# A planned mLSTM-and-two-layers kernel: another cutting of its first steps, two banks, one copy on another engine, other planner numbers

## The chip, the cores and the metric

The kernel runs on one core of one Trainium2 chip. The metric is the device time of one execution in microseconds, the median of several runs. Times inside the execution come from one profiled execution, counted from the start of its span.

## The reference

Three parts follow one another. An mLSTM attention (4 batches, 8 heads, 768 tokens, head size 40) is written as a recurrence over time; its output is a matrix of 3072 tokens by 320. Two feed-forward layers, 320 to 2048 to 320, follow, each with its own function between the two products. Gates and weights are scaled up by 8 to 64 in the inputs.

```python
for t in range(S):
    m_new = np.maximum(f_gate[:, :, t] + m, i_gate[:, :, t])
    f_stab = np.exp(f_gate[:, :, t] + m - m_new)
    i_stab = np.exp(i_gate[:, :, t] - m_new)
    m = m_new
    C = f_stab[:, :, None, None] * C + i_stab[:, :, None, None] * np.einsum('bhd,bhe->bhde', vt, kt)
    n = f_stab[:, :, None] * n + i_stab[:, :, None] * kt
    h_tilde = np.einsum('bhde,bhe->bhd', C, qt)
    nq = np.einsum('bhd,bhd->bh', n, qt)[:, :, None]
    y[:, :, t] = o * h_tilde / np.maximum(np.abs(nq), 1.0)

def _moe_ref(x, w_in, w_out):
    h = x @ w_in
    return ((h - np.tanh(h)) @ w_out).astype(np.float32)

def _moe2_ref(x, w_in, w_out):
    h = x @ w_in
    g = np.where(h >= 1, h, np.where(h <= -1, 0.0, (h + 1) ** 2 / 4))
    return (g @ w_out).astype(np.float32)
```

## The kernel before, in words

**Jobs.** The attention is cut into 24 jobs, each 128 tokens of one batch with all 8 heads (function `job`, L428). In a job the two halves of the heads are called u = 0 and 1. For each half a scan on VectorE (L489 for the first four jobs, L497 for the others) builds the decay matrix d from decay rows; from the fifth job on these rows are loaded by DMA from DRAM into the tile `fb`. The scan of the later jobs works in two diagonal blocks of 64; GpSimd copies one (L500), clears its place and fills the block below the diagonal. TensorE makes the scores of both halves into two PSUM banks (`t_s`, L516), VectorE multiplies them by d (L541), TensorE multiplies by the values and by the carried state C (`t_n`, L568 and L577), the result is normalised to x, transposed on TensorE (`t_x`, L606), and split for the layers into a high part (ScalarE, L656 and L660) and the rest (VectorE, L657 and L661). For the first four jobs a plain copy `xf` is kept as well (L642). For every fourth job the sigmoid of the o gate (L552) needs another table on ScalarE than the exponentials and tanh do.

**Layers.** Tokens go in six blocks of 512, the hidden width in 16 steps f of 128. In the first layer `step` (L689) multiplies the weights with x into a bank `h` (two banks, tag h), `activate` (L715) makes tanh on ScalarE (L725), the subtraction on VectorE (L726), the cast `gh` on ScalarE (L738) and the rest `gl` on VectorE (L739); `second` (L743) multiplies them with the second weights into four accumulators `a`, two steps later (LAG). Products are made from high and low parts (L707, L759). Only the first six steps of the first block (`WIDE`) use unsplit weights `wf` and x `xf` in one pass (L697), with the subtraction at L721. Steps zero and one of that block are issued in two column parts, 384 (the first three jobs) and 128 (the fourth); the later ones in one part of 512.

**Weights.** Each weight block of 704 columns comes as a load of 704 KB (`w64`) and is converted on ScalarE (L331) and VectorE (L333, L335), then split (L342, L344); that of the wide steps is split only later (`W_LATE`).

**What sets the order.** `Plan.schedule` is a list scheduler. Every instruction has a priority number (for the layers about the index of its step, for the jobs set by JOB0, AHEAD and others), a cost, and a margin that makes it count as finished later (LATE, or `margin` for a load). It takes what can start first, and by priority among what can start within PATIENCE; NEAR and FAR are the assumed delays from one engine to another. The result is a fixed order for each engine's queue. All loads go out on SyncE's queue (L296), in this order too. Where TensorE would wait in the planner's view, up to the end of step zero, it issues filler matmuls into a bank that nobody reads (`spare`, L853). PSUM banks are handed out by tag in the order in which the planner asks: for the later jobs `f` and `s0`, `s1` become the banks named in `jbank`, among them tn and tb, which the scores, t_x and others share in turn. A bank is free when its last reader is done.

## Time and profile before

| | us |
|---|---|
| median of 3 runs | 804.93 |
| lowest and highest | 803.73, 806.21 |
| profiled execution, its own time | 806.27 |
| span of that execution | 804.5 |
| TensorE busy (matmuls) in the span | 796.5 |
| VectorE, ScalarE, GpSimd busy | 556.8, 426.7, 201.1 |

Durations and starts below are from the profiled execution; its own time lies 1.8 us above its span. In a row of the timeline stand the start, the duration, the engine, the line and operation, output and input tiles with their partitions and elements, the number of instructions that were joined, and in brackets the idle time before with what ended it. The ends of matmuls are modelled, so two neighbours can overlap a little. In a list of waits stand, for an engine and line, what it waited for, and then the total, the number and the longest. TensorE's granted clock is 1.00 throughout, its higher level.

### The profile page before, as it was taken

To read this page: it belongs to the slowest core of one execution; us is meant where nothing else is said; L and a number is where in the kernel's file an instruction comes from. 1 tells how busy PE (TensorE), PEld (TensorE's weight loads), DVE (VectorE), ACT (ScalarE), POOL (GpSimd) and SP (SyncE) were. 2 spreads that over 40 slices of the span, in tenths; PEclk is the share of its full clock that TensorE was granted. 3 is DMA by queue.
4 is the path that set the end of the run, shared out by engine and by line. 5 is a ranking of instruction groups with operands and counts; after the bars stand their busy time and mean duration, and the time that the engine had idled before them with its cause. 6 is when DMAs were issued, how large, how long until landed. Compare 5 with 4: busy or idle time off the path is not lost.

```text
span 804.5 us, 15535 instructions
## 1 busy us (share of the span) xinstructions
PE 796.5 (99%) x6048; PEld 695.4 (86%) x6048; DVE 556.8 (69%) x931; ACT 426.7 (53%) x812; POOL 201.1 (25%) x268
## 2 busy tenths in 40 slices
PE   9999999999999999999999999999999999999998
PEld 6667889888988999889999898888989888898887
DVE  7998998888878888775456674746646566564644
ACT  4975685766776665443445543524435244342423
POOL 3245433656446554533100200200201002000000
PEclk9999999999999999999999999999999999999999
DMA  8998348887788576540543210100200000000000
GB/s 272 314 247 232 120 124 243 238 244 205 217 231 221 162 187 199 160 113 20 184 103 98 76 33 0 40 34 1 71 2 1 34 0 1 34 1 1 34 1 33
DMA packets 51300, 91.09 MB, mean 113 GB/s; under 512 B 5980, under 2 KB 33820, under 8 KB 51228
## 3 DMA queue, kind: packets, MB, share of 16 engines
q1 hardware_dynamic: 51180, 90.08, 39.4%
q8 instruction: 47, 0.77, 0.4%
q14 instruction: 25, 0.20, 0.1%
q10 hardware_dynamic: 48, 0.03, 0.0%
HBM read 76.26 MB, written 13.84 MB: 112 GB/s over the span
## 4 chain that ended last, share of the span: by engine, by line
PE 92%; DMA 3%; DVE 2%; ACT 2%; issue 0%; POOL 0%; POOLq 0%; DVEq 0%; ACTq 0%
PE a L759 40%; PE h L707 39%; DMA w<-in_w_dram 2%; PE t_n L577 2%; PE h L684 2%; PE t_c L613 2%; PE t_n L568 1%; PE t_s L537 1%; PE t_s L516 1%; PE spare L853 1%; PE t_f L477 1%; PE t_x L606 1%; DMA fb<-fr_d 1%; DVE w L344 1%; DVE w L333 0%
## 5 line engine op out<-in xcount | busy, mean ns | idle before, releaser
L707 PE MATMUL h<-x,w 128*128 128x512 f32 x1392 | 344.4, 396 | 0.7 <-DVE gl L739 0.7
L759 PE MATMUL a<-w,gh 128*128 128x320 f32 x1488 | 333.6, 311 | 0.0
L707 PEld LDWEIGHTS h<-x,w 128*128 128x128 f32 x1392 | 254.5, 188 | 58.3 <-issue 8.4
L759 PEld LDWEIGHTS a<-w,gh 128*128 128x128 f32 x1488 | 251.5, 188 | 6.8 <-issue 0.3
L759 PE MATMUL a<-w,gl 128*128 128x320 f32 x744 | 230.3, 310 | 0.0
L730 DVE TENSOR_SCALAR g<-h 128x512 f32<-128x512 f32 x96 | 65.8, 686 | 110.4 <-PE h L707 110.4
L732 ACT ACTIVATE g<-g,half 128x512 f32<-128x512 f32 x96 | 69.5, 724 | 136.8 <-DVE g L730 136.4
L759 PEld LDWEIGHTS a<-w,gl 128*128 128x128 f32 x744 | 139.7, 188 | 0.3
L823 POOL TENSOR_TENSOR x<-xl,x 128x512 fp32r<-128x512 f32 x18 | 26.8, 1512 | 275.2 <-ACT x L814 275.2
L726 DVE TENSOR_TENSOR h<-h,g 128x512 f32<-128x512 f32 x90 | 62.3, 693 | 32.7 <-ACT g L725 32.6
L725 ACT ACTIVATE g<-h 128x512 f32<-128x512 f32 x90 | 53.9, 599 | 56.8 <-PE h L707 56.5
L738 ACT CAST gh<-g 128x512 fp32r<-128x512 f32 x96 | 59.1, 616 | 46.1 <-DVE g L734 36.4
L739 DVE TENSOR_TENSOR gl<-g,gh 128x512 fp32r<-128x512 f32 x96 | 73.2, 782 | 10.7 <-ACT gh L738 10.7
L734 DVE TENSOR_TENSOR g<-h,g 128x512 f32<-128x512 f32 x96 | 65.5, 684 | 20.3 <-ACT g L732 20.3
L739 DVE TENSOR_TENSOR gl<-h,gh 128x512 fp32r<-128x512 f32 x90 | 61.1, 681 | 15.5 <-ACT gh L738 14.9
L738 ACT CAST gh<-h 128x512 fp32r<-128x512 f32 x90 | 52.3, 582 | 32.2 <-DVE h L726 23.3
L534 POOL TENSOR_TENSOR xf<-qkraw,xf 120x1024 fp32r<-120x1024 f32 x12 | 29.2, 2434 | 61.4 <-ACT xf L532 54.3
L497 DVE TENSOR_TENSOR_SCAN d<-fb,scan_id 128x256 f32<-128x256 f32 x40 | 34.3, 865 | 5.9 <-DMA fb<-fr_d 5.8
L532 ACT ACTIVATE xf<-qkraw,cs 120x512 fp32r<-120x512 f32 x48 | 32.5, 718 | 10.2 <-PE t_s L537 8.4
L541 DVE TENSOR_TENSOR d<-t_s,d 128x512 f32<-128x512 f32 x48 | 32.1, 681 | 5.9 <-PE t_s L537 5.0
L500 POOL COPY d<-d 64x256 f32<-64x256 f32 x40 | 21.5, 538 | 50.8 <-DVE d L497 48.0
L331 ACT ACTIVATE cvb<-w,half 128x704 bf16<-128x704 int8 x32 | 30.1, 941 | 4.5 <-DVE w L333 3.5
(113 smaller groups left out, 793.4 us busy)
## 6 DMA issues: line engine op xcount, KB each, us to landing
w<-in_w_dram SPq DMA_DIRECT2D x32, 703.6 KB
nat<-in_nat_dram SPq DMA_DIRECT2D x24, 484.0 KB
qkraw<-in_qk_dram SPq DMA_DIRECT2D x24, 480.0 KB
w_d<-w SPq DMA_DIRECT2D x16, 352.0 KB
w<-w_d SPq DMA_DIRECT2D x16, 352.0 KB
fb<-fr_d SPq DMA_DIRECT2D x40, 128.0 KB
qkraw<-in_qk_dram SPq DMA_DIRECT2D x24, 160.0 KB
xr_d<-xo SPq DMA_DIRECT2D x24, 160.0 KB
```

Of the source, the lines that this page charges most:

```text
L497: op("DVE", dve(512), p, lambda o=dk[u][0], i=f[u][0]: nc.vector.tensor_tensor_scan(out=o()[:, 0:HU * HL], data0=i(), data1=half_id, initi ...
L532: op("ACT", act(512, 1), at(u - 1), lambda raw=raw, t=t, z=z, cols=cols: nc.scalar.activation(t[:, cols], raw[:, cols], AF.Copy, scale=cs[ ...
L541: op("DVE", dve(512), at(2 + u), lambda p=sp[u], d=dk[u][0]: nc.vector.tensor_tensor(out=view(d()), in0=view(p.t, True), in1=view(d()), op ...
L707: op("PE", pe(n), prio, lambda i=i, c=c, s=s: nc.tensor.matmul(p[:, :n], w[:, c:c + 128], x[:, s, :n], start=(i == 0 and not layer), stop= ...
L725: op("ACT", act(n), prio + 0.5 - FFN, lambda: nc.scalar.activation(t[:, :n], p[:, :n], AF.Tanh), [p], [t])
L726: op("DVE", dve(n), prio + 0.5 - FFN, lambda: nc.vector.tensor_tensor(out=p[:, :n], in0=p[:, :n], in1=t[:, :n], op=ALU.subtract), [p, t], [p])
L730: op("DVE", dve(n), prio + 0.5 - FFN, lambda: nc.vector.tensor_scalar(t[:, :n], p[:, :n], -1.0, 1.0, op0=ALU.max, op1=ALU.min), [p], [t])
L732: op("ACT", act(n, 1), prio + 0.5 - FFN, lambda: nc.scalar.activation(t[:, :n], t[:, :n], AF.Square, bias=half[:, 0:1], scale=0.5), [t, "h ...
L734: op("DVE", dve(n), prio + 0.5 - FFN, lambda: nc.vector.tensor_tensor(out=t[:, :n], in0=p[:, :n], in1=t[:, :n], op=ALU.max), [p, t], [t])
L738: op("ACT", act(n), prio + 1 - FFN, lambda: nc.scalar.copy(gh[:, :n], y[:, :n]), [y], [gh])
L739: op("DVE", dve(n), prio + 1 - FFN, lambda: nc.vector.tensor_tensor(out=gl[:, :n], in0=y[:, :n], in1=gh[:, :n].bitcast(F32), op=ALU.subtra ...
L759: op("PE", pe(DM) if gl is not None else 2 * pe(DM, 128, 2), prio, lambda A=A, r=r, a=a, c=c, i=i, dt=dt: nc.tensor.matmul(A[:, 0:DM], a[: ...
```

## The change

Step zero of the first layer's first block is issued in three column parts (0 to 256, 256 to 384, 384 to 512), steps one and two in two (384 and 128). Steps two and three write the banks tn and tb, taken once after the fourth job's last use, instead of the two h banks. The copy of the diagonal block (L500) is made by ScalarE, at a slightly later priority. Loads of a job may be issued four steps ahead of it (LOADS) instead of two; the wide steps' weights are split two steps earlier (W_LATE) in priority, the first conversion starts one earlier (W_CONV); the assumed delay to TensorE and GpSimd's lateness are smaller (FAR, LATE); second-layer weights count as landing later, and the jobs' loads have a margin of 1600 from the seventh job on instead of 2500 from the ninth.

```diff
-AHEAD, LOADS = 7, 2
+AHEAD, LOADS = 7, 4
-SPLIT = 2
-W_LATE = 15
+CUTS = ((2, 3), (3,), (3,))
+HX = {2: 'tn', 3: 'tb'}
+W_LATE = 13
-W_CONV = [-14, -10, -7, -5, -3, -2, -1]
+W_CONV = [-15, -10, -7, -5, -3, -2, -1]
-    NEAR, FAR, PE_OUT = 80.0, 160.0, 170.0
+    NEAR, FAR, PE_OUT = 80.0, 130.0, 170.0
-    LATE = {"POOL": 0.3, "DVE": 0.05, "ACT": 0.1}
+    LATE = {"POOL": 0.2, "DVE": 0.05, "ACT": 0.1}
...
-             704, w=[t], rows=5629, margin=3000.0 if layer else 0.0)
+             704, w=[t], rows=5629, margin=6000.0 if layer else 0.0)
...
-        load(ld, lambda: nt.t, lambda: nat[b, c * L:(c + 1) * L], 484, w=[(nt, 0), (nt, 1), (nt, 2)], rows=3872, margin=2500.0 if n >= 8 else 0.0)
+        load(ld, lambda: nt.t, lambda: nat[b, c * L:(c + 1) * L], 484, w=[(nt, 0), (nt, 1), (nt, 2)], rows=3872, margin=1600.0 if n >= 6 else 0.0)
...
-            op("POOL", 380, p + 0.25, lambda ds=ds: nc.gpsimd.tensor_copy(ds()[HL:128, 1], ds()[HL:128, 0]), [Z], [D_C])
+            op("ACT", act(256), p + 0.3, lambda ds=ds: nc.scalar.copy(ds()[HL:128, 1], ds()[HL:128, 0]), [Z], [D_C])
...
-        p = None if layer else bank("h", "h")
+        p = None if layer else free.pop((k, f), None) or bank("h", "h")
         if wide(layer, k, f):
             w, x = wf[f], xf[0]
-            cut = BLK[0] - 1 if f < SPLIT else 0
-            for a, b in ((0, cut), (cut, BLK[0])) if cut else ((0, BLK[0]),):
+            cuts = (0, *(CUTS[f] if f < len(CUTS) else ()), BLK[0])
+            for a, b in zip(cuts, cuts[1:]):
                 for i in range(3):
...
     jobs(0)
+    free.update({(0, f): bank(t, "h") for f, t in HX.items()})
```

The line with `nat` stands for the same edit on `fb`, `gb` and `q3`. Lines of the changed kernel are one higher than those of the kernel before, from about L878 two.

The first place is TensorE's order from the last scores of the fourth job (`t_s`) on; `spare` are the fillers, `h_...` with `wf_284` is step zero, with `wf_386` step one, `t_x` the transposes of the third job and then of the fourth. Before (the pair of weight load and filler stands here once, and is there eight times):

```order
L516 MATMUL t_s_445<-qkraw_198 128x128
L853 LDWEIGHTS gh_88
L853 MATMUL spare_101<-gh_88 128x512
...
L606 MATMUL t_x_480<-cs_72,x_107 128x128 x3
L577 MATMUL t_n_494<-nat_211,d0_389 32x41 x32
L613 MATMUL t_c_531<-nat_211 120x123 x2
L697 MATMUL h_539<-xf_334,wf_284 128x384 x2
L606 MATMUL t_x_550<-cs_72,x_107 128x128 x3
L697 MATMUL h_539<-xf_334,wf_284 128x384
L697 MATMUL h_562<-xf_334,wf_386 128x384
L697 MATMUL h_539<-xf_334,wf_284 128x128 x3
...
L697 MATMUL h_589<-xf_334,wf_470 128x512 x3
```

And in the changed kernel:

```order
L517 MATMUL t_s_445<-qkraw_199 128x128
...
L854 MATMUL spare_101<-gh_88 128x512
L698 MATMUL h_470<-xf_334,wf_284 128x256 x3
...
L607 MATMUL t_x_485<-cs_72,x_107 128x128 x3
L578 MATMUL t_n_492<-nat_211,d0_389 32x41 x32
L614 MATMUL t_c_529<-nat_211 120x123 x2
...
L698 MATMUL h_470<-xf_334,wf_284 128x128 x3
L698 MATMUL h_546<-xf_334,wf_386 128x384
L607 MATMUL t_x_551<-cs_72,x_107 128x128 x3
...
L698 MATMUL h_577<-xf_334,wf_473 128x384 x3
```

The first 256 columns of step zero moved ahead of the third job's transposes, between two fillers where there were eight; the next 128 follow them, the last 128 follow those of the fourth.

The second place is VectorE's order at the seventh job (job six, counted from zero). `d_...<-fb_...` is a scan, `t_x` the split of the job before, `h` the subtraction after tanh, `d_...<-t_s_...` the multiplication of the scores. Before:

```order
L497 SCALAR_TENSOR_TENSOR d_1073<-fb_978,scan_id_73 128x256
L657 TENSOR_TENSOR x1_893<-t_x_1060,x1_893 128x2x128
L661 TENSOR_TENSOR x1_893<-t_x_1060,x1_893 64x128
L726 TENSOR_TENSOR h_1034<-h_1034,g_1081 128x512
L335 SCALAR_TENSOR_TENSOR w32_864<-w64_721,w32_864 128x704
L497 SCALAR_TENSOR_TENSOR d_1114<-fb_1025,scan_id_73 128x256
L541 TENSOR_TENSOR d_980<-t_s_1099,d_980 128x512
L739 TENSOR_TENSOR gl_1129<-h_1034,gh_1110 128x512
```

And in the changed kernel:

```order
L727 TENSOR_TENSOR h_1014<-h_1014,g_1049 128x512
L498 SCALAR_TENSOR_TENSOR d_1077<-fb_937,scan_id_73 128x256
L658 TENSOR_TENSOR x1_882<-t_x_1065,x1_882 128x2x128
L662 TENSOR_TENSOR x1_882<-t_x_1065,x1_882 64x128
L345 TENSOR_TENSOR w10_1026<-w32_781,w10_1026 128x704
L336 SCALAR_TENSOR_TENSOR w32_933<-w64_734,w32_933 128x704
L542 TENSOR_TENSOR d_1021<-t_s_1100,d_1021 128x512
L740 TENSOR_TENSOR gl_1130<-h_1014,gh_1084 128x512
L345 TENSOR_TENSOR w11_1123<-w32_933,w11_1123 128x704
L542 TENSOR_TENSOR d_1077<-t_s_1099,d_1077 128x512
...
L498 SCALAR_TENSOR_TENSOR d_1199<-fb_1073,scan_id_73 128x256
```

The multiplication of job six's first half (L542, d_1021) stood behind the first scan of job seven (L497, d_1114), and now stands ahead of it; the subtraction moved ahead of the other scan.

The third place is SyncE's queue of loads ahead of that. Before, `w64_929` is the last first-layer weight block, `fb_978` the decay rows of job six's second half and `fb_1025` those of job seven's first:

```order
L296 DMA fb_883<-fr_d_78 64x2x256
...
L296 DMA nat_910<-in_nat_dram 128x968
L296 DMA w64_929<-in_w1_dram 128x5629
L296 DMA fb_978<-fr_d_78 64x2x256
L296 DMA fb_978<-fr_d_78 64x256
L296 DMA q3_989<-in_q3_dram 120x384
L296 DMA qkraw_999<-in_qk_dram 40x1024 x2
L296 DMA fr_1018<-in_fg_dram 32x128
L296 DMA fb_1025<-fr_d_78 64x2x256
```

In the changed kernel the same are `w64_995`, `fb_937` and `fb_1073`, and `w64_1042` is the first second-layer block:

```order
L297 DMA nat_924<-in_nat_dram 128x968
L297 DMA fb_937<-fr_d_78 64x2x256
L297 DMA fb_937<-fr_d_78 64x256
...
L297 DMA q3_983<-in_q3_dram 120x384
...
L297 DMA w64_995<-in_w1_dram 128x5629
L297 DMA fr_1028<-in_fg_dram 32x128
...
L297 DMA w64_1042<-in_w2_dram 128x5629
L297 DMA fb_1073<-fr_d_78 64x2x256
```

The weight block moved behind the decay rows of job six, and a second-layer block moved ahead of those of job seven.

## Rows read from the trace of the kernel before

**Rows 1.** Page, busy time, share of the span and instructions of each engine.
```profile
PE 796.5 (99%) x6048; PEld 695.4 (86%) x6048; DVE 556.8 (69%) x931; ACT 426.7 (53%) x812; POOL 201.1 (25%) x268
```
**Rows 2.** Windows: length, busy us of each engine (instructions), clock, DMA share, GB/s.
```profile
40.00:50.00 10.00, 10.00 (x43) 5.70 (x42) 9.87 (x12) 7.70 (x13) 5.26 (x8) 1.00 0.80 202
60.00:70.00 10.00, 9.41 (x53) 7.08 (x52) 8.84 (x19) 5.67 (x14) 6.58 (x11) 1.00 1.03 270
70.00:80.00 10.00, 9.11 (x116) 7.83 (x117) 7.25 (x16) 6.32 (x16) 4.42 (x7) 1.00 0.77 195
500.00:600.00 100.00, 100.00 (x562) 88.17 (x562) 58.98 (x88) 41.51 (x67) 9.39 (x6) 1.00 0.09 30
```
**Rows 3.** Timeline of TensorE, 25 to 38 us: start, us, instructions, [idle before].
```profile
25.48 1.90 PE L853 MATMUL spare<-gh 128*128 128x512 bf16 x8
...
35.10 2.84 PE L697 MATMUL h<-xf,wf 128*128 128x512 f32 x6 [0.21 <-DVE gh L721]
37.78 2.32 PE L759 MATMUL a<-wf,gh 128*128 128x320 f32 x8
```
**Rows 4.** Timeline of VectorE, 24 to 51 us.
```profile
24.27 1.06 DVE L335 SCALAR_TENSOR_TENSOR wf<-w,wf 128x704 int32<-128x704 int32 x1
...
34.36 0.68 DVE L721 TENSOR_TENSOR gh<-h,g 128x512 f32<-128x512 f32 x1
...
48.59 2.41 DVE L344 TENSOR_TENSOR w<-wf,w 128x704 fp32r<-128x704 f32 x1
```
**Rows 5.** TensorE's list of waits, whole run: total us, times, longest.
```profile
PE spare L853 <- POOL gh L856: 1.3, 1, 1.3
...
PE h L697 <- DVE gh L721: 0.2, 1, 0.2
```
**Rows 6.** Timeline of TensorE, 67 to 121 us, its four larger waits.
```profile
67.05 1.25 PE L516 MATMUL t_s<-qkraw 40*128 40x128 f32 x16 [0.59 <-issue]
...
79.75 1.25 PE L516 MATMUL t_s<-qkraw 40*128 40x128 f32 x16 [0.85 <-issue]
...
83.42 0.87 PE L568 MATMUL t_n<-C,q 120*128 120x123 f32 x6 [0.69 <-POOL d L500]
...
119.14 2.11 PE L707 MATMUL h<-x,w 128*128 128x512 f32 x8 [0.65 <-DVE gl L739]
```
**Rows 7.** Timeline of VectorE, 65 to 84 us.
```profile
65.05 0.69 DVE L497 TENSOR_TENSOR_SCAN d<-fb,scan_id 128x256 f32<-128x256 f32 x1 [1.08 <-DMA fb<-fr_d]
...
66.67 0.28 DVE L661 TENSOR_TENSOR x<-t_x,x 64x128 fp32r<-64x128 f32 x1
...
78.34 0.69 DVE L497 TENSOR_TENSOR_SCAN d<-fb,scan_id 128x256 f32<-128x256 f32 x1 [1.16 <-DMA fb<-fr_d]
...
79.36 0.28 DVE L661 TENSOR_TENSOR x<-t_x,x 64x128 fp32r<-64x128 f32 x1
...
82.04 0.69 DVE L497 TENSOR_TENSOR_SCAN d<-fb,scan_id 128x256 f32<-128x256 f32 x1 [0.70 <-DMA fb<-fr_d]
82.65 0.67 DVE L541 TENSOR_TENSOR d<-t_s,d 128x512 f32<-128x512 f32 x1
```
**Rows 8.** Timeline of ScalarE, 64 to 119 us.
```profile
64.88 0.37 ACT L656 CAST x<-t_x 128x256 fp32r<-128x256 f32 x1 [0.27 <-PE t_x L606]
...
115.29 1.28 ACT L552 ACT_TABLE_LOAD   x1
...
117.78 0.57 ACT L738 CAST gh<-h 128x512 fp32r<-128x512 f32 x1
```
**Rows 9.** Timeline of SyncE's DMA issues, 67 to 72 us.
```profile
67.64 0.36 SPq L296 DMA_DIRECT2D w<-in_w_dram  x1
70.57 1.25 SPq L296 DMA_DIRECT2D fb<-fr_d  x2
```
**Rows 10.** Page, costliest groups: busy us, mean ns, idle before with its releaser.
```profile
L500 POOL COPY d<-d 64x256 f32<-64x256 f32 x40 | 21.5, 538 | 50.8 <-DVE d L497 48.0
```
**Rows 11.** VectorE's list of waits, 40 to 130 us.
```profile
DVE d L497 <- DMA fb<-fr_d: 4.7, 5, 1.2
```

More of the change, by code (lines that the diff above doesn't have):

```diff
@@ L451, in job @@
                              "w h t -> w (h t)").unsqueeze(0).to_broadcast([HL, w, HU * HL]),
-                         kb, r=[("fr_d", kc, v) for v in ((0, 1) if a == 0 else (2,))], w=[(ft, a)], rows=512, margin=2500.0 if n >= 8 else 0.0)
+                         kb, r=[("fr_d", kc, v) for v in ((0, 1) if a == 0 else (2,))], w=[(ft, a)], rows=512, margin=1600.0 if n >= 6 else 0.0)
                 f[u] = lambda ft=ft: ft[:, 0:HU * HL], [(ft, 0), (ft, HL)]
@@ L460, in job @@
                     c, b * H:(b + 1) * H].unsqueeze(0)[:, i:H:3].to_broadcast([D, m, L]),
-                    20 * m, r=[("gr_d", kc)], w=[(g, i)], rows=512, margin=2500.0 if n >= 8 else 0.0)
+                    20 * m, r=[("gr_d", kc)], w=[(g, i)], rows=512, margin=1600.0 if n >= 6 else 0.0)
             G = [(g, i) for i in range(3)]
             q = abuf("q3", [120, 3, L], F32, 1)
-            load(ld + 0.8, lambda: q.t, lambda: q3[b, c], 180, w=[(q, 0), (q, 1)], rows=1536, margin=2500.0 if n >= 8 else 0.0)
+            load(ld + 0.8, lambda: q.t, lambda: q3[b, c], 180, w=[(q, 0), (q, 1)], rows=1536, margin=1600.0 if n >= 6 else 0.0)
         dk, pk, bc = {}, {}, []
@@ L662, in split_x @@
             out=t[64:128, 4, cols], in0=r(), in1=t[0:64, 4, cols].bitcast(F32), op=ALU.subtract), [*src, (t, key, 2)], [(t, key, 2)], lock=lock or eng == "POOL")
-    acc = {}
+    acc, free = {}, {}
     def xkeys(layer, k, j):
```

## The prediction

> **What bounds the kernel now.** The page comes first: TensorE is busy 99% of the span [rows 1]. That figure hides two regimes, so the windows by stage come next. From 500 to 600 us TensorE is busy all 100 us while VectorE has 59 and ScalarE 42 [rows 2]: there the matmuls themselves are the time, and the change neither adds nor removes one of them. Before about 120 us it is otherwise: VectorE is busy 9.87 of 10 us at 40 to 50, the DMA engines are full (share 1.03 at 60 to 70, still 0.77 at 70 to 80), and TensorE has holes [rows 2]. So what the change can win is what TensorE loses before 120 us, and it reaches the end only if TensorE stays ahead until then.
>
> The losses are read from TensorE's timeline. First, from 25.48 for 1.90 us it runs eight filler matmuls, 0.22 us each, while it waits for the transposed x of the third job [rows 3]. Second, step two (its records have 512 columns) starts at 35.10 us with 0.21 us idle, released by VectorE's subtraction of step zero, which ran from 34.36 for 0.68 us [rows 3, 4]. Printed idle counts from the modelled end of the last matmul, and that end overlaps the next start by 0.16 us where nothing waits (35.10 + 2.84 = 37.94 against a start at 37.78 [rows 3]); so each wait costs its idle plus 0.16: here 0.37. Third come four larger waits. The list of TensorE's waits over the whole run has five entries: one of 1.3 us ahead of the program's first filler, which the change does not touch, the 0.2 of step two, and these four [rows 5, 6]: 0.59, 0.85, 0.69 and 0.65 idle, with the overlap 0.75, 1.01, 0.85 and 0.81 us.
>
> Their causes are on VectorE [rows 7]. The scores at 67.05 need both score banks; the last one is freed by the x split that ended at 66.67 + 0.28 = 66.95, and that split stood behind a scan that had waited 1.08 us for its decay rows (the tile fb) until 65.05. The scores at 79.75 follow the split that ended at 79.64, behind a scan that waited 1.16 us for fb until 78.34. The t_n matmul at 83.42 is put down to a GpSimd copy of d, which it does not read; it needs the first score bank, freed by the multiplication at 82.65 + 0.67 = 83.32, which stood behind a scan of the next job that waited 0.70 us for fb. So three of the four are fb landing late in front of an in-order queue. The fourth, at 119.14, is released by gl of step zero of the second block; ahead of it ScalarE loaded a table from 115.29 for 1.28 us and cast gh only at 117.78 [rows 8].
>
> **Step zero in three parts.** Its first 256 columns now run in the filler gap, as the first order fence shows. Half of a step of 2.68 us (35.10 to 37.78 [rows 3]) is 1.34, and six fillers at 0.22 were 1.33, so the transposes still start where they did: they wait for x anyway. The weight block must be there: its last conversion ends at 24.27 + 1.06 = 25.33 [rows 4], 0.37 us before the one filler left in front ends at 25.70. Gain: **1.3 us**. The further cuts cost nothing that I can see; they are the same columns.
>
> **Step two in a bank of its own.** It need not wait for step zero's subtraction, which ended at 35.04 [rows 4]; its weights and x are converted before, since nothing of that moved. Gain: **0.4 us** (0.37). In exchange the scores of job four, in the same two banks, come after step three. They wait for nothing there, and their readers ran late anyway, so nothing.
>
> **First late scan (67.05).** The DMA engines are full there, so I leave the landing at 65.05. In the new order the scan is followed at once by the x split (the second fence shows the same pattern a job later), without the 0.6 us of subtraction between: the scores can start near 66.5. Four matmuls of a step are moved ahead of them, 0.24 us each ((2.11 - 0.16)/8 at 119.14 [rows 6]), which TensorE can do while it waits. Started 0.55 us earlier with 1.0 us more work behind it, TensorE keeps its lead of about 1.6 and wins nothing: **0**, between 0.75 won (fb earlier) and 0.75 lost.
>
> **Second and third late scan (79.75, 83.42).** The third fence shows the queue of loads: the last weight block of 704 KB, before issued at 67.64 ahead of the scan's fb at 70.57 [rows 9], now goes behind it. At the 270 GB/s of 60 to 70 [rows 2] that is 2.6 us; fb lands near 75.7 instead of 78.3 and the scan does not wait: **1.0 us**. The multiplication that frees the bank for t_n now stands ahead of the next job's scan: **0.85 us**. Bounds of the two together: 0 (fb no earlier) and 1.9.
>
> **VectorE's load.** The split of w1 moves out of 48.59, where it took 2.41 us [rows 4], to about 110. VectorE was full there, so up to 2.4 us come free. That is the cover of the gains: a TensorE 3.5 us ahead asks for everything that much earlier, through 80 to 112, and if the cover is too thin, the leads shrink. I take **0.5 us lost**, between 0 and 2.
>
> **Copy on ScalarE.** Forty copies leave GpSimd (21.5 us, mean 538 ns [rows 10]) for ScalarE. ScalarE's nearest row, a cast of 256 columns, takes 0.37 us [rows 8]; eight copies before 105 us are 3 us in a stretch where it is busy 6.32 of 10 [rows 2]. Nothing by itself, between the 4.3 us that eight at GpSimd's mean would take out of ScalarE's slack and the gain of the second rival. But ScalarE's queue now holds the tanh and gh casts behind a copy that waits for the scan, so a late fb stops two engines instead of one (the third rival).
>
> **Table loads.** The new order has twelve on ScalarE where it had ten: in the second token block a sigmoid now falls between the two exponentials of one gate group. A load is 1.28 us [rows 8], so the pair adds 2.6 us to an engine with room, and one of the two stands between a tanh and its cast like that at 115.29, which cost TensorE 0.81. I take **0.4 us lost**, between 0 and 0.8. The fourth wait, 0.81, stays: the same table load stands in the same place.
> The Trainium skill (ScalarE: Activation LUTs, What ACT_TABLE_LOAD costs) says that a switch costs about 2.66 us, the load and as long again for a drain. By that rule the pair would add 5.3 us of ScalarE, the loss would nearer double to 0.8 and the sum fall to 2.2; no row here shows a drain.
>
> **Other planner margins** move loads and jobs against each other after 130 us; there TensorE has no wait at all in the list [rows 5], so nothing, within 0.5 either way.
>
> Sum: 1.3 + 0.4 + 0 + 1.0 + 0.85 - 0.5 - 0.4 = 2.65, rounded 2.6. The profiled execution took 806.27 us, its span 804.5; it is 1.3 above the median of 804.93. Its span would be 801.9; against the median **802.3 us**.
>
> **Rivals.**
> *The change does not do what it says.* If the weight block were late, step zero's first part would wait in the gap in place of the fillers and 1.3 us would go. The 0.37 us above speaks against it; I give it no chance of its own, but it lies inside the range (803.6).
>
> *The loads set the pace.* The DMA engines are full at 60 to 70 [rows 2], and a faster TensorE only meets the same landing times. For it: three of the four waits are loads. Against it: the share falls to 0.77 at 70 to 80, and what was late was the order. Then all that was won before 88 us shrinks to what lies in the queue's order, 0.5 to 1: 804.2 us.
>
> *VectorE gains more.* GpSimd's copies have a mean of 0.54 us [rows 10] beside VectorE's work, and the split at 48.59 took 2.41 us for 704 columns where the two-input multiplication at 82.65 took 0.67 for 512 [rows 4, 7]. If each of the eight copies before 105 us gives VectorE its 0.54 us back, 4.3 us come free on an engine that is full there, and about 2 of them reach TensorE as the waits that I left in: 800.3 us. The Trainium skill (SBUF — State Buffer, SBUF: two separate sides) says that VectorE and GpSimd share one port pair under an exclusive lock, and that ScalarE's ports are never waited for. By that rule the gain is this rival's; the rows show one stretched instruction, and not what stretched it.
>
> *ScalarE becomes the bound (slower).* The copy waits for the scan and the scan for fb, and behind it in ScalarE's queue stand tanh and gh, which free the h banks. If fb lands no earlier than before, the five waits of the scans between 40 and 130 us, 4.7 us together [rows 11], all reach TensorE in place of the 2.6 that do now, and the 1.7 won before is met by the same landings. With both prices of the table pair (0.8) the sum is -1.3 - 0.4 + 2.1 + 1.7 + 0.8 = 2.9 slower: 807.8 us. It decides when a copy waits longer than ScalarE's slack to the next tanh, about a microsecond.
>
> **How the numbers follow.** A measurement of this kernel can tell about 0.3% from no change, 2.4 us: faster means under 802.5. My forecast has 0.50; its own range is 801 to 803.7, a little over half of it under the line. The pace of the loads has 0.30, the freed VectorE 0.14, ScalarE 0.06. Faster: 0.27 + 0.14 + 0.05 (the lower edge of the second) = 0.46. Slower 0.06, the same 0.48. The range goes from 800.3 (the VectorE rival) to 805.2 (the loads' rival and a microsecond of unseen waits).
>
> **What would show it.** Right: two fillers between the third job's scores and x, the first part of step zero at 25.7 us, the first second-layer matmul (a) near 36.1 instead of 37.78; the scan of job six not waiting for fb; no idle before the scores and t_n of that job. Wrong: scans that still wait 1 us for fb, ScalarE idle before the copy of d with a tanh behind it, TensorE idle at 90 to 110 released by VectorE's gl or splits, or a new wait at the added table loads.

## The result, and the profile after

The changed kernel takes **810.45 us** (median of 6 runs, 807.91 to 814.74), the kernel before 804.44 in the runs beside it: a ratio of **1.0070** (1.0051 to 1.0088). Forecast were 802.3, and 800.3 to 805.2. The direction is wrong, and the time lies outside the range. The ratios in this document are those on record, from runs of both kernels made beside each other; a ratio of the two medians (here 1.0075) can differ from them by up to 0.0008. One run in this document, of e9 below (821.77 us), was in a slow state and counts in no median or ratio. The profiled execution took 809.99 us, 808.2 of them span.

The page looks as before, but for the forty copies that changed engine and the two table loads that came to ScalarE:

```profile
PE 795.3 (98%) x6051; PEld 695.8 (86%) x6054; DVE 561.5 (69%) x931; ACT 445.3 (55%) x854; POOL 184.4 (23%) x228
```

The early part went as forecast. TensorE's timeline of the changed kernel, the stretch of [rows 3]:

```profile
24.69 1.13 PE L517 MATMUL t_s<-qkraw 40*128 40x128 f32 x15
25.98 1.46 PE L698 MATMUL h<-xf,wf 128*128 128x256 f32 x6 [0.16 <-issue]
27.27 0.38 PE L854 MATMUL spare<-gh 128*128 128x512 bf16 x1
27.53 0.55 PE L607 MATMUL t_x<-cs,x 128*128 128x128 f32 x3
...
31.10 5.40 PE L698 MATMUL h<-xf,wf 128*128 128x384 f32 x28
36.34 0.97 PE L760 MATMUL a<-wf,gh 128*128 128x320 f32 x3
```

The first part of step zero fills the gap, step two waits for nothing, and the first second-layer product (a) starts at 36.34 in place of 37.78. TensorE's whole list of waits, which answers to [rows 5], tells where this went:

```profile
PE t_s L517 <- issue: 1.9, 2, 1.0
PE t_n L569 <- issue: 1.7, 2, 1.3
PE t_x L607 <- DVE x L603: 1.5, 2, 0.9
PE spare L854 <- POOL gh L857: 1.3, 1, 1.3
PE t_s L538 <- DVE xf L535: 1.3, 1, 1.3
PE h L708 <- DVE gl L740: 0.6, 1, 0.6
PE t_n L578 <- issue: 0.3, 1, 0.3
PE h L698 <- issue: 0.2, 1, 0.2
```

The waits of t_x and of the later jobs' scores (t_s, L538) were not in the list before. On the timeline the waits behind 120 us are these, where the kernel before had none over 0.04:

```profile
153.78 0.87 PE L569 MATMUL t_n<-C,q 120*128 120x123 f32 x6 [1.27 <-issue]
...
166.29 0.87 PE L569 MATMUL t_n<-C,q 120*128 120x123 f32 x6 [0.41 <-issue]
...
258.21 0.66 PE L538 MATMUL t_s<-xf 120*128 120x128 f32 x4 [1.32 <-DVE xf L535]
...
268.77 0.52 PE L607 MATMUL t_x<-cs,x 128*128 128x128 f32 x3 [0.95 <-DVE x L603]
...
304.91 0.52 PE L607 MATMUL t_x<-cs,x 128*128 128x128 f32 x3 [0.54 <-DVE x L603]
```

Windows by token block, before and then after (columns as in [rows 2]; the limits are where each block's second-layer products begin):

```profile
120.00:199.00 79.00, 78.96 (x788) 69.98 (x787) 66.93 (x134) 50.93 (x116) 43.58 (x66) 1.00 0.84 234
199.00:271.00 72.00, 72.00 (x674) 64.95 (x673) 60.28 (x109) 50.80 (x108) 35.71 (x49) 1.00 0.78 217
271.00:342.00 71.00, 71.00 (x664) 64.10 (x663) 57.52 (x99) 43.89 (x92) 34.39 (x47) 1.00 0.63 175
```

```profile
120.00:199.00 79.00, 77.31 (x779) 68.21 (x778) 66.46 (x127) 55.92 (x127) 37.58 (x53) 1.00 0.75 208
199.00:274.00 75.00, 72.59 (x673) 64.58 (x672) 60.91 (x108) 53.15 (x115) 31.41 (x39) 1.00 0.72 197
274.00:346.00 72.00, 71.46 (x667) 64.42 (x667) 61.60 (x104) 50.45 (x106) 32.28 (x40) 1.00 0.74 210
```

VectorE is busy 81 to 86% in all six. In the kernel before, TensorE never waits there all the same. The first second-layer product of the second block and the last matmul of the program, before and then after:

```profile
121.09 0.45 PE L759 MATMUL a<-w,gh 128*128 128x320 f32 x2
...
800.69 0.31 PE L759 MATMUL a<-w,gl 128*128 128x320 f32 x1
```

```profile
118.90 0.45 PE L760 MATMUL a<-w,gh 128*128 128x320 f32 x2
...
804.18 0.31 PE L760 MATMUL a<-w,gl 128*128 128x320 f32 x1
```

So the reading is: the second block's products begin 2.2 us ahead; from there to the end of the last matmul it takes 685.6 us in place of 679.9, **5.7 us more**. The five waits behind 120 us have 4.5 us of idle; with the 0.16 of overlap that the prediction adds to each they are 5.3, nearly all of it.

The queues beside each wait tell where it comes from. Ahead of 153.78, 268.77 and 304.91 a scan on VectorE takes 2.8 to 2.9 us in place of 0.68, while GpSimd runs its long subtraction (L535). At 153.78 VectorE's multiplication of the scores, for which TensorE waits, stands right behind the scan. At the other two ScalarE's copy waits for the scan, a tanh stands behind the copy, and VectorE waits 1.42 us for the tanh. VectorE, ScalarE and GpSimd of the changed kernel, at the first place and the last:

```profile
150.31 2.78 DVE L498 TENSOR_TENSOR_SCAN d<-fb,scan_id 128x256 f32<-128x256 f32 x1
153.02 1.25 DVE L542 TENSOR_TENSOR d<-t_s,d 128x512 f32<-128x512 f32 x2
...
297.22 2.79 DVE L498 TENSOR_TENSOR_SCAN d<-fb,scan_id 128x256 f32<-128x256 f32 x1
...
301.73 0.70 DVE L727 TENSOR_TENSOR h<-h,g 128x512 f32<-128x512 f32 x1 [1.42 <-ACT g L726]
```

```profile
300.05 0.40 ACT L501 COPY d<-d 64x256 f32<-64x256 f32 x1 [1.49 <-DVE d L498]
...
301.10 0.60 ACT L726 ACTIVATE g<-h 128x512 f32<-128x512 f32 x1
```

```profile
150.15 2.40 POOL L535 TENSOR_TENSOR xf<-qkraw,xf 120x1024 fp32r<-120x1024 f32 x1 [1.15 <-DVE gl L740]
...
296.61 2.86 POOL L535 TENSOR_TENSOR xf<-qkraw,xf 120x1024 fp32r<-120x1024 f32 x1 [9.00 <-ACT xf L533]
```

At 258.21 it is a small load of a gate: VectorE waits 2.00 us for it, with the subtraction that TensorE needs queued behind.

```profile
256.56 0.48 DVE L366 TENSOR_TENSOR_SCAN mg<-fr,carry,ig 32x128 f32<-32x128 f32 x1 [2.00 <-DMA ig<-in_ig_dram]
256.97 1.19 DVE L535 TENSOR_TENSOR xf<-qkraw,xf 120x1024 fp32r<-120x1024 f32 x1
```

### The profile page after: what moved, and what is told of

Same layout as the page of the kernel before. It is cut to its first block, busy times and chain, and to the rows that moved or that the text cites. A ratio compares the mean times of both kernels' runs of the same rounds, so it can differ in the third digit from the quotient of the medians.

```text
span 808.2 us, 15597 instructions
## 1 busy us (share of the span) xinstructions
PE 795.3 (98%) x6051; PEld 695.8 (86%) x6054; DVE 561.5 (69%) x931; ACT 445.3 (55%) x854; POOL 184.4 (23%) x228
## 4 chain that ended last, share of the span: by engine, by line
PE 87%; DVE 5%; DMA 3%; ACT 3%; issue 2%; SPq 0%; POOL 0%; DVEq 0%; POOLq 0%; ACTq 0%
PE a L760 38%; PE h L708 37%; DMA w<-in_w_dram 2%; PE h L685 2%; PE t_n L578 2%; PE t_c L614 1%; PE t_n L569 1%; PE t_s L517 1%; PE t_s L538 1%; PE t_x L607 1%; PE t_f L478 1%; DVE d L498 1%; DVE gl L740 1%; PE spare L854 1%; DMA ig<-in_ig_dram 1%
## 5 line engine op out<-in xcount | busy, mean ns | idle before, releaser
L535 POOL TENSOR_TENSOR xf<-qkraw,xf 120x1024 fp32r<-120x1024 f32 x12 | 29.6, 2469 | 57.1 <-ACT xf L533 26.6
L498 DVE TENSOR_TENSOR_SCAN d<-fb,scan_id 128x256 f32<-128x256 f32 x40 | 39.3, 994 | 2.2 <-DMA fb<-fr_d 2.0
L542 DVE TENSOR_TENSOR d<-t_s,d 128x512 f32<-128x512 f32 x48 | 32.1, 682 | 5.6 <-PE t_s L538 5.1
L503 POOL TENSOR_TENSOR d<-fb,d 64x256 f32<-64x256 f32 x40 | 27.1, 682 | 35.6 <-DVE d L498 17.0
L549 POOL TENSOR_TENSOR nat<-nat,isT 128x328 f32<-128x328 f32 x24 | 21.2, 892 | 50.6 <-DMA nat<-in_nat_dram 36.5
```

Source lines behind the costliest of these rows:

```text
L498: op("DVE", dve(512), p, lambda o=dk[u][0], i=f[u][0]: nc.vector.tensor_tensor_scan(out=o()[:, 0:HU * HL], data0=i(), data1=half_id, initi ...
L542: op("DVE", dve(512), at(2 + u), lambda p=sp[u], d=dk[u][0]: nc.vector.tensor_tensor(out=view(d()), in0=view(p.t, True), in1=view(d()), op ...
```

## The experiments

Six theories on where the 5.7 us come from stood against each other:

- **A**: the copy blocks ScalarE, and the tanh behind it comes late.
- **B**: the planner's new numbers put GpSimd's long subtraction beside VectorE's scans, which it holds up.
- **C**: the early lead only meets work that is late.
- **D**: any new order of the planner loses behind 120 us, whatever made it.
- **E**: it is the content of the change (its copy, banks and margins).
- **F**: the changed kernel's order is an unlucky one, and the change is good in most.

The readings first, one profile each. "Moved" counts those of VectorE's 933 planned instructions that stand elsewhere in its queue than in the kernel before. "Gap" runs from the third job's transposes to the first second-layer product, "block one" is the start of that block's second-layer products, "rest" the time from there to the end of the last matmul. The ratio is to the runs of the kernel before made beside. A profile is one execution: the third job's transposes, which wait for VectorE and not for an edited place, start at 27.26 in the kernel before and between 26.71 and 28.09 in the four kernels that keep VectorE's order, so a microsecond in the column "block one" says little.

| kernel | moved | gap | block one | rest | ratio (95%) |
|---|---|---|---|---|---|
| before | 0 | 10.52 | 121.09 | 679.9 | 1 |
| e7_part_by_hand | 0 | 10.51 | 118.37 | 680.3 | 1.0008 (0.9986 to 1.0029) |
| e12_hand_and_load | 0 | 10.51 | 119.06 | 681.2 | 1.0012 (0.9994 to 1.0030) |
| e13_hand_bank | 0 | 9.50 | 118.32 | 682.0 | 1.0005 (0.9993 to 1.0017) |
| e2_copy_alone | 0 | 10.52 | 121.80 | 684.4 | 1.0050 (1.0032 to 1.0068) |
| e5_nudge_far | 70 | 10.52 | 117.99 | 682.0 | 1.0018 (1.0000 to 1.0036) |
| e11_banks_alone | 78 | 10.04 | 121.09 | 681.3 | 1.0019 (0.9998 to 1.0039) |
| e6_nudge_near | 79 | 10.52 | 121.12 | 681.9 | 1.0035 (1.0016 to 1.0054) |
| e10_large_nudge_b | 198 | 10.80 | 117.52 | 687.7 | 1.0039 (1.0021 to 1.0058) |
| changed kernel | 215 | 8.81 | 118.90 | 685.6 | 1.0070 (1.0051 to 1.0088) |
| e8_halves | 215 | 8.81 | 118.26 | 685.6 | 1.0037 (1.0019 to 1.0054) |
| e1_copy_back | 215 | 8.81 | 117.93 | 688.2 | 1.0093 (1.0073 to 1.0113) |
| e9_large_nudge_a | 220 | 10.80 | 119.06 | 684.9 | 1.0065 (1.0042 to 1.0088) |
| e14_nudge_halves | 220 | 10.79 | 119.81 | 692.4 | 1.0142 (1.0114 to 1.0171) |
| e4_numbers_alone | 224 | 10.52 | 123.35 | 687.5 | 1.0097 (1.0074 to 1.0121) |
| e3_parts_alone | 232 | 8.81 | 118.27 | 691.3 | 1.0105 (1.0089 to 1.0120) |
| e15_change_nudged | 265 | 8.78 | 118.01 | 690.2 | 1.0115 (1.0093 to 1.0136) |

**The change taken apart.** *e1_copy_back*: the changed kernel's order, the copy issued on GpSimd.

```diff
-            op("ACT", act(256), p + 0.3, lambda ds=ds: nc.scalar.copy(ds()[HL:128, 1], ds()[HL:128, 0]), [Z], [D_C])
+            op("ACT", act(256), p + 0.3, lambda ds=ds: nc.gpsimd.tensor_copy(ds()[HL:128, 1], ds()[HL:128, 0]), [Z], [D_C])
```

The planner still lays the copy out as ScalarE's; only the engine that runs it differs.

> The changed kernel with its order on every queue kept, only that the forty copies of d are issued on GpSimd at the same place of the order. Theory A (ScalarE's queue stands behind the copy, which waits for a scan; tanh comes after it): TensorE's waits at about 269 and 305 us (0.95 and 0.54 idle) go, those near 154 and 166 shrink, and the time falls by 2 to 4 us, to 806.5 to 808.5. Theory B (the planner's new numbers put long GpSimd work beside the scans and loads too late; the copy matters little): the scans of 2.8 us stay, and the time stays within 1 us of 810.4. If the copy on GpSimd stretches VectorE's work, it would be slower than 810.4.

812.6 us, a ratio of 1.0093 in place of 1.0070: no gain. The waits at 268.77 and 304.91 are gone, as theory A has it, but new ones of 1.35 and 2.40 us stand at 173.4 and 178.0. Moving the copy back takes away the waits that A blames, and not the loss.

*e2_copy_alone*: the order before, the copy issued on ScalarE.

```diff
-            op("POOL", 380, p + 0.25, lambda ds=ds: nc.gpsimd.tensor_copy(ds()[HL:128, 1], ds()[HL:128, 0]), [Z], [D_C])
+            op("POOL", 380, p + 0.25, lambda ds=ds: nc.scalar.copy(ds()[HL:128, 1], ds()[HL:128, 0]), [Z], [D_C])
```

> The kernel before with its order on every queue kept, only that the forty copies of d are issued on ScalarE at the same place of the order. Theory A (the copy blocks ScalarE): 2 to 4 us slower, 806.5 to 808.5, with TensorE waits after 130 us that the kernel before has not. Theory B (planner numbers): within 1 us of 804.4, no new wait over 0.3 us after 130 us.

809.97 us, 0.5% slower, a little over theory A's range: with every other place kept, the forty copies alone, at places in ScalarE's queue that were planned for GpSimd, lose 4.5 us behind 120 us in this profile. Of the waits that the kernel before had not, two:

```profile
78.91 0.52 PE L606 MATMUL t_x<-cs,x 128*128 128x128 f32 x3 [1.23 <-DVE x L602]
...
239.72 0.64 PE L537 MATMUL t_s<-xf 120*128 120x128 f32 x4 [1.48 <-DVE x L661]
```

But the first is not a copy in the way: VectorE's split (L344) took 2.65 us there. In the second ScalarE had waited 1.97 us for a write to DRAM, and the copy of 0.40 us stood between that and the cast for L661. Taken with e1, one reading, argued and not shown, is that a queue that was in step for one set of durations is out of step for another, in both directions.

*e3_parts_alone* and *e4_numbers_alone*: the kernel before with the parts and banks (CUTS, HX and their lines of the diff), or with the planner numbers alone, planned anew (the scheduler ran again and could place every instruction elsewhere).

```diff
-SPLIT = 2
+CUTS = ((2, 3), (3,), (3,))
+HX = {2: 'tn', 3: 'tb'}
...
```

> The kernel before with the column parts and the two banks alone, planned anew with the old numbers. Theories A and B both expect the gain of the prediction's first two steps, 1.3 + 0.4 us, so 802.5 to 803.2, with six fillers fewer. A third theory C (TensorE ahead by 1.7 us only meets later work that is late) expects no gain, 804 to 805, with the waits near 67 to 83 us larger by what was won.

```diff
-AHEAD, LOADS = 7, 2
+AHEAD, LOADS = 7, 4
-    NEAR, FAR, PE_OUT = 80.0, 160.0, 170.0
+    NEAR, FAR, PE_OUT = 80.0, 130.0, 170.0
...
```

> The kernel before with the planner's new numbers alone (loads earlier, smaller delays and margins), planned anew. Theory B: 3 to 6 us slower, 807 to 810, with scans of over 2 us beside GpSimd's long subtraction and TensorE waits between 130 and 310 us. Theory A: within 1.5 us of 804.4.

814.12 and 813.75 us: each alone costs more than all together. None of A, B and C has room for the first. B expected the second to be slower, though not by as much, but the scans are shorter here than in the kernel before (30.8 us in sum, before 34.3). Costs that don't add up led to theory D.

**Nudges.** *e5_nudge_far* and *e6_nudge_near* change nothing but the order, in places.

```diff
-    NEAR, FAR, PE_OUT = 80.0, 160.0, 170.0
+    NEAR, FAR, PE_OUT = 80.0, 158.0, 170.0
```

> The kernel before with one planner number moved by next to nothing: the assumed delay to TensorE is 158 ns in place of 160. Nothing that is computed or issued changes, only the order in places. Theory D (the order of the kernel before is a fitted one that loses nothing after 130 us, and nearly any other order that the planner makes loses 3 to 8 us there): 807 to 812 us, with several TensorE waits of 0.5 to 2 us between 130 and 360 us. Theories A and B (the copy, or the size of the new numbers, does the harm): within 1.5 us of 804.8.

```diff
-    NEAR, FAR, PE_OUT = 80.0, 160.0, 170.0
+    NEAR, FAR, PE_OUT = 81.0, 160.0, 170.0
```

> The kernel before with the assumed delay between the other engines at 81 ns in place of 80. Theory D: 807 to 812 us, with TensorE waits between 130 and 360 us at other places than in the other nudge. Theories A and B: within 1.5 us of 804.8. If one nudge costs and the other does not, the loss depends on the draw.

806.24 and 808.16 us, 0.2 and 0.35% slower, with 2 us lost in the rest. The first is below D's range and its interval reaches down to no change; the second is inside it. These two move a third of what the change moves; *e9_large_nudge_a* and *e10_large_nudge_b* move as much.

```diff
-    NEAR, FAR, PE_OUT = 80.0, 160.0, 170.0
+    NEAR, FAR, PE_OUT = 79.0, 160.0, 170.0
```

> The kernel before with the assumed delay between engines at 79 ns in place of 80. Nothing that is computed changes, but the order does as much as in the changed kernel: 220 of VectorE's 933 instructions and 240 of ScalarE's 815 stand elsewhere (changed kernel 215 and 206; the two nudges tried so far 70 to 79). Theory D (the price of a new order, whatever made it): 808 to 814 us, with 3 to 6 us of TensorE idle between 130 and 360 us. Theory E (it is the content of the change, its copy, banks and smaller margins): 805 to 807.5, like the small nudges.

```diff
-    return 157 + n / 0.96
+    return 158 + n / 0.96
```

> The kernel before with every VectorE instruction costed 1 ns higher by the planner, which moves 198 of VectorE's and 233 of ScalarE's instructions. Theory D: 808 to 814 us, with waits at other places than in the first large nudge. Theory E: 805 to 807.5 us.

811.04 and 809.41 us, a ratio of 1.0065 and 1.0039 for one nanosecond, both in D's range. The changed kernel's 1.0070 is of the same size as the first and above the second. E, which had 805 to 807.5 for both, falls as it was put.

*e11_banks_alone* moves as little as a small nudge.

```diff
+HX = {2: 'tn', 3: 'tb'}
...
-        p = None if layer else bank("h", "h")
+        p = None if layer else free.pop((k, f), None) or bank("h", "h")
...
+    free.update({(0, f): bank(t, "h") for f, t in HX.items()})
```

> The kernel before with steps two and three in banks of their own and nothing else, planned anew; this moves 78 of VectorE's instructions, as few as the small nudges. Prediction's second step: TensorE's wait at 35.1 us (0.21 idle) goes, 0.4 us won early. Theory D: the new order costs as much as a small nudge, so 805 to 808. Theory E with the banks at fault (job four's scores come later): over 809, with waits at the scores between 45 and 70 us.

807.0 us (0.9998 to 1.0039). The gap is 0.5 us shorter, near the 0.4 of the prediction's second step, and 1.4 us go in the rest. That is D's range, and no bank is at fault.

*e15_change_nudged* is the changed kernel with the edit of e10.

> The changed kernel, all its parts kept, with every VectorE instruction costed 1 ns higher by the planner: 196 of VectorE's and 132 of ScalarE's instructions stand elsewhere than in the changed kernel. Theory D: one more draw of an order that nobody fitted, 808 to 814 us, with the first 36 us as in the changed kernel, and 3 to 8 us lost between 120 and 350 us at other places. Theory F (the changed kernel's own order is an unlucky one, and the change is good in most): 802 to 805.

814.84 us, with the gap at 8.78: the early gain is there, and 10.3 us go in the rest. F expected 802 to 805. One more draw is no proof for all, but it is slower still, and no run bears F out.

**The order kept.** *e7_part_by_hand*: the planner's result for the kernel before, edited by hand.

```diff
     P.schedule()
+
+    def forward():
...
+        first.allocs.remove(p)
+        gap.allocs.append(p)
+        gap.fill, rest = 0, gap.fn
+
+        def go():
+            filler(1)
+            for i in range(3):
+                nc.tensor.matmul(p[:, 0:256], w[:, i * 128:(i + 1) * 128].bitcast(F32), x[:, i, 0:256], start=(i == 0), stop=(i == 2))
+            filler(1)
+            rest()
+
+        gap.fn = go
...
```

> The kernel before with its order on every queue kept, only that the first 256 columns of step zero are issued in place of six of the eight filler matmuls (the planner's result is edited by hand, nothing is planned anew). Prediction's first step (1.3 us won, and kept to the end): the second-layer matmuls of step zero start near 36.5 in place of 37.78 us, the span ends 1.3 us earlier, 803.2 to 803.8. Theory C (the lead meets work that is late): start as said, but the waits at 67 to 84 us grow by as much, 804.5 to 805.3. Theory D in its strong form (any shift in time disturbs the fitted order): new waits after 130 us, above 805.5.

805.78 us, no change: 1.3 us less would be a ratio of 0.9984, just outside the interval. The part sits in the gap, and its 1.3 us are gone ten microseconds later: TensorE waits 0.5 us for the fourth job's x and 0.8 in place of 0.2 for step two's bank. That is theory C, earlier than it was put.

```profile
PE h L704 <- DVE gh L728: 0.8, 1, 0.8
PE h L714 <- DVE gl L746: 0.7, 1, 0.7
PE t_x L606 <- DVE x L597: 0.5, 1, 0.5
PE t_i L383 <- DVE x L661: 0.3, 1, 0.3
PE t_n L568 <- issue: 0.2, 1, 0.2
PE t_s L516 <- issue: 0.2, 1, 0.2
```

The list shows a second thing. The waits at 67 to 83 us, 0.59, 0.85 and 0.69 in [rows 6], are here none, 0.2 and 0.2, with the same loads in the same order. This execution took 803.91 us, 1.9 less than the median of its kernel.

*e13_hand_bank* gives step two the bank tn besides.

```diff
+        early[-1].tag, early[-1].cap = "tn", 1
```

> The kernel with the first part of step zero issued by hand in the filler gap, and step two written by hand into the bank tn; every place in every queue as in the kernel before. By the first two terms of the prediction, and as the changed kernel itself showed (1.7 us from the third job's transposes to the first second-layer matmul): that stretch takes 8.8 us in place of 10.5, the wait before step two (0.75 idle in the run by hand without the bank) goes. Theory D (an order that is kept loses next to nothing after 120 us): less than 1.5 us is lost behind 120 us, the time is 803 to 805, below or at the kernel before. Against it: the lead of 1.7 us moves TensorE against the other queues, and 3 us or more are lost behind 120 us, over 807.

805.59 us, no change. The gap is 9.50 and not the expected 8.8: 1.0 us shorter, with the wait for the fourth job's x still there (0.5). Then the microsecond is lost again at one place, to VectorE's multiplication of the scores, which starts at 54.35 in the kernel before and at 54.54 here:

```profile
55.32 0.87 PE L568 MATMUL t_n<-C,q 120*128 120x123 f32 x6 [1.01 <-issue]
```

In the kernel before the same matmul starts at 55.13 without a wait. The rest takes 682.0, 2.1 us more in this profile, where the expectation had under 1.5.

*e12_hand_and_load*: e7, and the last weight load issued behind job six's decay rows.

```diff
+    late_w, fb = mark['w', 0, NF - 1], mark['fb', 6, 1]
+    i, j = P.ops.index(late_w), P.ops.index(fb)
...
+    P.ops.insert(j + 1, late_w)
+    del P.ops[i]
```

> The kernel with the first part of step zero issued by hand in the filler gap, and besides the last first-layer weight load issued behind the decay rows of job six in place of ahead of them; every other place in every queue as in the kernel before. Prediction's third step (1.0 us won at 79.75 and up to 0.85 at 83.42 by the earlier rows): the scan of job six's second half does not wait for its rows, the waits of TensorE near 78 and 81 us go, median 803 to 804.5, below the kernel before. If the DMA engines set the pace: the scan waits as before and the time stays at 805 to 806.

The waits for the scores and t_n of [rows 6] are gone; VectorE's own list, 40 to 130 us, has one wait for decay rows in place of the five of [rows 11]:

```profile
DVE d L499 <- DMA fb<-fr_d: 0.7, 1, 0.7
```

806.97 us, no change (0.9994 to 1.0030), so the gain of 1 to 2.5 us that was expected is not there. In e7, with the loads in the old order, two of these waits were 0.2 us each, so little was left to win.

**GpSimd's long subtraction.** *e8_halves* (in the changed kernel) and *e14_nudge_halves* (in e9) issue it in two parts.

```diff
+                def diff(e, raw=raw, t=t, m=2 if u == 0 else 1):
+                    for z in range(m):
+                        c = slice(z * 1024 // m, (z + 1) * 1024 // m)
+                        e.tensor_tensor(out=t[:, c], in0=raw[:, c], in1=t[:, c].bitcast(F32), op=ALU.subtract)
```

> The changed kernel with its order on every queue kept, only that GpSimd's long subtraction of scores data (1024 columns, 2.4 us) is issued as two of 512 columns. Theory B (VectorE's scans are held by that instruction for as long as it runs): scans that begin beside it take at most 1.7 us in place of 2.8, the waits at 153.8 and 304.9 us shrink by about 1 us in sum or more, 808 to 809.5. Otherwise the scans stay at 2.8 us and the time within 1 us of 810.4.

> The first large nudge (79 ns in place of 80) with its order kept, only that GpSimd's long subtraction is issued in two halves. Theory B as part of D (a scan that begins beside that instruction is held till its end, and a new order brings them together): scans of 2.5 to 2.8 us become at most 1.8, and the time falls by 1.5 to 3 us from 811.9, to 809 to 810.5. If the gain of the halves in the changed kernel was chance: 811 to 813.

The scans do what theory B says. Shortest, median and longest in ns, in the changed kernel, in e8, in e9 and in e14:

```profile
L498 DVE TENSOR_TENSOR_SCAN d<-fb,scan_id x40: 653/680/2889, 43.8 to 365.8; 128x256 f32<-128x256 f32 x40
```

```profile
L498 DVE TENSOR_TENSOR_SCAN d<-fb,scan_id x40: 653/681/1776, 44.9 to 365.2; 128x256 f32<-128x256 f32 x40
```

```profile
L497 DVE TENSOR_TENSOR_SCAN d<-fb,scan_id x40: 649/681/2817, 45.3 to 365.5; 128x256 f32<-128x256 f32 x40
```

```profile
L497 DVE TENSOR_TENSOR_SCAN d<-fb,scan_id x40: 649/682/1770, 44.5 to 373.7; 128x256 f32<-128x256 f32 x40
```

In both the longest scan fell by about 1.1 us, but the time does not follow it. e8 took 808.91 us, 0.33% less than the changed kernel in relation to the kernel before, as theory B expected; e14 took 816.97, 0.8% more than e9, where B expected a gain. In e8's profile the waits at the three places shrink (0.97 in two, 0.68 and 0.27 in place of 1.27, 0.95 and 0.54), while new ones of 1.43 and 1.04 us stand at 136.2 and 176.4. So the hold is real, and part of the changed kernel's loss may be its price; it is not the price of a new order in general.

None of the kernels beats the kernel before; the three that keep its order are level with it.

## Why the prediction was wrong, point by point

- *Step zero in three parts, step two's bank: 1.3 + 0.4 = 1.7.* Right: 10.52 to 8.81, 1.71 us, and the same 8.78 to 8.81 in all five kernels that have both. But the two are not independent, as they were priced: the part alone, the order kept, gives nothing (e7), with the one bank 1.0 (e13).
- *First late scan: 0.* Right within its bounds. The wait is there at 66.90, with 0.99 idle in place of 0.59.
- *Second and third late scan: 1.85.* The waits are gone in the changed kernel, yet the term was wrong in kind: waits of one execution were priced as a loss of every execution. They are 0.2 us or none in e7 and e13 too, with the loads in the old order, and taking the cause away wins nothing (e12). The one execution that was profiled, at 806.27 us, was slower than each of the three runs known then.
- *VectorE's load: 0.5 lost, between 0 and 2.* Right in kind: a new wait for scores at 97.56 of 0.89, with VectorE 9.88 us busy from 90 to 100.
- *Table loads: 0.4 lost.* The wait of 0.41 at 166.29 follows one of them, and the size is right.
- Sum at the start of block one: forecast 3.05 without the tables, measured 2.2 in one profile each.
- *Copy on ScalarE: nothing.* Wrong. The copy's own size was right (0.40 against 0.37), but the forecast asked only whether ScalarE had room. In the old order, at places planned for GpSimd, it loses 4.5 us (e2); in the new order, moving it back wins nothing (e1). What it costs in the new order is not known.
- *Other planner margins:* **"there TensorE has no wait at all in the list [rows 5], so nothing, within 0.5 either way" is the step that failed**, by 5.7 us (whatever the copy costs there included). No wait in the list was read as slack. But VectorE is busy 81 to 86% of that stretch with its queue in a fixed order, and a scan held for 2 us or a load 2 us late reaches TensorE. Of the nine orders that the planner made anew, the six that move 198 instructions or more lose 5.0 to 11.4 us there, nudges of one nanosecond among them; the three that move 70 to 79 lose 1.4 to 2.1; the three kernels that keep order and engines lose 0.4 to 2.1, and their medians are level with the kernel before. These are readings of one profile each, in which the small losses are no more than the runs of one kernel differ.
- *Rivals.* The one that ended slower gave 807.8 by a copy that waits behind a scan in front of tanh. That chain is in the profile (1.49 at 300.05), but the scan was late beside GpSimd, not for its rows, and e1 takes the chain away without a gain. It was right in sign for a reason that did not hold. No rival said that a new order has a price of its own.

Shown: that an order moved as far as this costs 0.39 and 0.65% without any edit, where the change costs 0.70%. Not shown: how much of the changed kernel's 5.7 us is the new order and how much its edits. The two large nudges lie below all four orders that hold edits (the changed kernel, e3, e4 and e15: 1.0070 to 1.0115), so a price of the edits themselves is not excluded; but e14, the order of a nudge with the subtraction halved, lies above them all. Whether the order before loses nothing by choice or by chance, and whether the change would win the 1.7 us if its planner numbers were searched until an order fits, was not tried.

## What to carry to other kernels

Where a planner writes the order, a change has two prices: that of the edit, and that of a new order. Measure the second by itself, with a nudge that means nothing and moves as many instructions, before the first is believed; and test an edit with every place in every queue kept. A stretch without waits need not be slack when the engine beside it is as busy as here (81 to 86%). A wait in one profile is a gain only if other executions have it too.

## What the runs showed of the hardware

A wait of TensorE can cost twice. In e3_parts_alone it waited 1.92 us until 182.46; from there the granted clock was 0.50, the lower level of 1.2 GHz, and seven matmuls took 3.36 us, 0.48 each in place of 0.24. Windows of that kernel, then its timeline:

```profile
176.00:180.00 4.00, 4.00 (x25) 3.60 (x24) 1.33 (x3) 1.11 (x2) 0.72 (x2) 1.00 1.02 353
183.00:186.00 3.00, 3.00 (x8) 2.32 (x8) 1.77 (x4) 0.00 (x0) 1.95 (x2) 0.50 0.79 193
187.00:190.00 3.00, 3.00 (x21) 2.78 (x20) 2.84 (x5) 3.00 (x5) 1.26 (x1) 1.00 0.82 300
```

```profile
182.46 0.22 PE L384 MATMUL t_i<-cs,ig 32*128 32x32 f32 x1 [1.92 <-DVE x L662]
182.61 3.36 PE L708 MATMUL h<-x,w 128*128 128x512 f32 x7
```

The same followed a wait of 2.06 us in e4, and in e14 one of 2.90, where the clock was 0.50 from 190 to 196. The length of the wait does not settle it: in e1 one of 2.40 us at 178.0 left the clock at 1.00, and in e6 one of 0.81 at 20.1 was followed by 0.50 from 22 to 25. In the changed kernel's profile the longest wait behind the start was 1.32 and the clock 1.00 up to the last matmul; its slowest run, 814.74 us, had a mean clock of 0.997. By an estimate from that, 0.003 of a span of 813 us, the lower level cost it up to 2.4 us. It does not order the runs: that of 810.39 has 0.997 too.

A scan that takes 0.68 us alone takes up to 2.89 when it begins beside GpSimd's subtraction, and at most 1.78 when that is issued in halves. In the changed kernel's profile seven scans begin while the subtraction runs; they take 1.08 to 2.89 us, and each ends 0.54 or 0.55 us after it does. The Trainium skill (SBUF — State Buffer, SBUF: two separate sides) says that VectorE, in an instruction with two inputs in SBUF as the scan has, and GpSimd share a port pair that the first to start holds for its whole instruction. The seven ends and the rows of the four kernels above agree with it.
